# The first product of a row block pair in seven smaller ones, and a new order around it

## The chip, the cores and the metric

The kernel runs on one core of one Trainium2 chip. The metric is device time in microseconds of one execution; for the kernel before it is the median of three runs, 787.54 us (787.51 to 788.31). A separate execution was recorded by the hardware profiler; all durations below come from that one.

## The reference

Four sequences of 768 rows go through hash-bucketed attention (8 heads of 64), whose heads side by side are the 512 columns of x, and then through an MLP mixer:

```python
xt = x.transpose(0, 2, 1)
h = np.maximum(xt @ w_tok1, 0.0) @ w_tok2
u = x + h.transpose(0, 2, 1)
h2 = np.maximum(u @ w_ch1, 0.0) @ w_ch2      # 512 -> 1536 -> 512
return (u + h2).astype(np.float32)
```

Everything here concerns the first matrix product of the last step, u @ w_ch1, with the relu that follows. All data are float32.

## The kernel before

Attention fills the first 310 us, the token mixing runs to 388 us, and the rest is the channel part, `channels`. It works on XT, which holds u transposed: 128 partitions of columns by 4 blocks of columns by 3072 rows. The rows are taken in three row block pairs s = 0, 1, 2, each of two blocks of TT = 512 rows.

For each pair the product with w_ch1 is made by Winograd's form of a 2x2 block product: seven products p1 to p7 in place of eight, with sums of the blocks of the right side (the rows: T, made by `inputs`) and of the left side (the weights: SW1). For s = 1 and 2 most of the seven are themselves made in seven smaller ones. Class `Smaller` does that. Its `left` holds seven weight blocks of 128x128, its `b` eight blocks of 128x256 of the rows: four raw ones and four sums, which `right_sums` makes on VectorE with four subtractions. The seven matmuls of 256 columns come in three calls:

- `one(pair, e)`: one matmul into the first quarter of a pair of PSUM banks; `keep` copies it into `e` (ScalarE)
- `rest()`: three matmuls, of which the first adds onto that same quarter; `unite()` copies it again (ScalarE), and `add()` makes the other quarters (VectorE)
- `three(pair)`: three matmuls that go straight into the pair in which the whole product is wanted; `seed()` first copies the kept parts back into that pair (ScalarE)

`used()` runs after `three` and after `rest`, and when both are done, it asks for the next weight blocks of that product by a transfer on SP's queue.

The six blocks of 128 hidden columns of a row half are taken as three tiles t = 0, 1, 2 (GP = 3). `hidden_first(s, 0, ...)` does t = 0, `hidden_pair(s, t)` the others, then `outputs(s)` makes the product with w_ch2 by seven calls, `whole_product` and six of `product`, the last of them `product(s, 6, "p4", ...)`. All engines execute their instructions in the order in which these functions list them; there is no scheduler. A pair of PSUM banks is a tile with one buffer, taken anew by `bank_pair(i)`; there are four, whose order `ring` holds. `product` takes the first two of the ring and moves them to its end, so that `hidden_first` finds the pairs of the last product but one as x and z, and those of the last product as e and y.

Before, p1 for t = 0 is not made in smaller products: `opened` (L1036) makes it with four matmuls of 512 columns into X, and only its later tiles are `Smaller`, begun ahead by `open_next`. Their left sums are made once, by `sum_first_left` (L897) at the end of the third `product` of s = 0.

The right sums for a pair are made on VectorE: those of p2 and p3 already within `outputs(s - 1)`; those of p5 and p6 ahead of `hidden_first`; those of p7, p4 and p1 inside it, where it calls `between[0]` to `between[2]`. The lines that call it:

```python
for s in range(1, last + 1):
    for name in ("p5", "p6"):
        right_sums(name, s)[0]()
    hidden_first(s, 0, [right_sums(name, s)[0] for name in ("p7", "p4", "p1")])
```

A look (`look`, or `begin_look` and `end_look`) is work from another part of the kernel that is spread over these stages: two passes of ScalarE over 128x768 numbers of an input, which POOL's queue then follows with the load of a next one.

Of the kernel before, what the change touches and what calls it, by code (L numbers as in the profile page):

```python
# [48 lines left out]
def kernel(  # L49
# [705 lines left out]
    def channels(pool, psum, SW1, second, TA, judge):  # L755
# [15 lines left out]
        def bank_pair(i):  # L771
            return psum.tile([P, 2, TT], F32, name=f"b{i}", tag=f"b{i}", bufs=1)
# [7 lines left out]
        def accumulate(ps, left, right, ks, start=True, stop=True):  # L780
            ks = list(ks)
            for k in ks:
                nc.tensor.matmul(  # L783
                    ps, left(k), right(k), start=start and k == ks[0], stop=stop and k == ks[-1],
                    skip_group_check=True,
                )
# [101 lines left out]
        def fifth_left():  # L888
            return SW1[:, 1].rearrange("p k c -> p (k c)")[:, 2 * TT : 2 * TT + 4 * P]

        def first_left_sums():

            return [
                SW1[:, ::2].rearrange("p i k c -> p i (k c)")[:, :, P * (7 + i) : P * (8 + i)] for i in range(4)
            ]

        def sum_first_left():  # L897
            (a00, a01), (a10, a11) = [
                [a[:, 0, P:].rearrange("p (t c) -> p t c", c=P) for a in half]
                for half in weight_quarters(first_weight("p1"))  # L900
            ]
            new = first_left_sums()
            nc.vector.tensor_tensor(new[1], a00, a10, op=ALU.subtract)
            nc.vector.tensor_tensor(new[0], a10, a11, op=ALU.add)
            nc.vector.tensor_tensor(new[2], new[0], a00, op=ALU.subtract)
            nc.vector.tensor_tensor(new[3], a01, new[2], op=ALU.subtract)

        def hidden_left_at(h):

# [5 lines left out]
        def weight_quarters(w):  # L915
            k, c = w.shape[1] // 2, w.shape[2] // 2
            return [[w[:, :k, cs], w[:, k:, cs]] for cs in (slice(0, c), slice(c, 2 * c))]

        def first_weight(name):

            return {
                "p2": WC1[:, KC:, : DCH // 2], "p3": SW1[:, 2], "p4": WC1[:, KC:, DCH // 2 :], "p6": SW1[:, 0],
                "p5": WC1[:, :KC, DCH // 2 :], "p7": SW1[:, 1], "p1": WC1[:, :KC, : DCH // 2],
            }[name]
# [5 lines left out]
        class Smaller:  # L930


            def __init__(self, h, name, s, t):
                self.h, self.name, self.s, self.t, self.fetched = h, name, s, t, False
                self.b = right_sums(name, s)[1]
                if h is None:
                    raw = [a for b in weight_quarters(first_weight(name)) for a in b]
                    raw = [raw[i][:, 0, P * t : P * t + P] for i in (0, 1, 3)]
                    if name == "p1":
                        sums = [a[:, t - 1] for a in first_left_sums()]  # L940
                    else:
                        sums = [fifth_left()[:, P * i : P * i + P] for i in range(4)]
                    self.left = [*sums, *raw]
                else:
                    w = hidden_left_at(h).rearrange("p (i c) -> p i c", i=7)
                    self.left = [w[:, i] for i in range(7)]
# [75 lines left out]
        def plus(to, a, b):  # L1022
            nc.vector.tensor_tensor(to, a, b, op=ALU.add)  # L1023
# [4 lines left out]
        def relu(a):  # L1028
            nc.scalar.activation(a, a, ACT.Relu)

        def whole(pair, left, right, which, t):
            for i in which:
                at = P * (t + GP * i)
                accumulate(pair[:, i], lambda k: left(k)[:, at : at + P], right, range(KC))

        def opened(pair, which, s, t):  # L1036
            start = TT * 2 * s
            whole(pair, lambda k: WC1[:, k], lambda k: XT[:, k, start : start + TT], which, t)

        def open_next(bank, s, t):  # L1040
            p1 = Smaller(None, "p1", s, t + 1)
            p1.pair = bank_pair(bank)
            p1.one(p1.pair, left_at(7 * s + 1)[:, 2 * TT : 4 * TT])
            ahead.append(p1)

        def bounds(r):
# [10 lines left out]
        def hidden_first(s, t, between):  # L1057


            r, (p2, p6, p7, p3, p4) = parts_of(s, t)  # L1060
            x, z, e, y = ring
            ring[:] = [y, e, z, x]
            p1, e4, e2, e3 = [flat(output_at(i)) for i in range(4)]
            e7 = flat(q1)
            e5, e6, u = copies(), copies(), copies()
            p5 = Smaller(None, "p5", s, t)
            n = TT * 3 // 2

            X = bank_pair(x)
            opened(X, [0, 1], s, t)  # L1070
            look()
            Z, E = bank_pair(z), bank_pair(e)
            p2.one(E, e2)
            copy_pair(p1, X)
            p2.three(Z, True)
            Y = bank_pair(y)
            p5.one(Y, e5)
            begin_look()
            plus(p1[:, :n], flat(Z)[:, :n], p1[:, :n])
            between[0]()  # L1080
            p2.rest()
            p2.unite()
            end_look()
            p2.add()
            p5.rest()
            p5.unite()
            p5.add(True)
            p6.three(X)
            p6.one(bank_pair(z), e6, False)
            copy_pair(u, X)  # L1090
            p6.keep()
            p5.seed()
            plus(r[0], rows(p1), rows(e2))
            V = bank_pair(e)
            between[1]()
            p7.three(V, True)
            p6.rest()
            p6.finish()
            plus(u, u, e6)
            p7.one(bank_pair(x), e7)  # L1100
            p5.three(Y)
            p5 = e5
            copy_pair(p5, Y)
            p7.rest()
            plus(p5[:, :n], flat(V)[:, :n], p5[:, :n])
            p7.finish()
            p3.one(bank_pair(z), e3)
            p3.three(Y)
            relu(r[0])
            p4.three(V)  # L1110
            p4.one(bank_pair(x), e4)
            p3.rest()
            plus(r[1], banks(Y), rows(u))
            plus(u, u, e7)
            plus(r[2][:, 0], banks(V)[:, 0], rows(u)[:, 0])
            plus(r[2][:, 1, 0], banks(V)[:, 1, 0], rows(u)[:, 1, 0])
            between[2]()
            p3.finish()
            nc.scalar.copy(r[2][:, 1, 1], rows(u)[:, 1, 1])
            open_next(y, s, t)  # L1120
            p4.rest()
            p4.finish()
            later(1, "p6", lambda: plus(r[3], rows(p5), rows(u)))
            later(1, "p3", lambda: plus(r[1], r[1], rows(e3)))
            later(1, "end", lambda: relu(r[3]))
            later(2, "p2", lambda: plus(r[2], r[2], rows(e4)))
            later(2, "u", *bounds(r))
            later(2, "end", lambda: relu(r[2]))
# [105 lines left out]

        SMALLER = ["p2", "p6", "p7", "p3", "p4"]
        GP = HC // 2
        ahead, postponed, slots, finished = [], [], {}, [0]
        hidden_passed = second["hidden_passed"]


# [85 lines left out]
        def left_at(g):  # L1326
            return area(g % 2)[:, : 7 * QC * P]
# [143 lines left out]
        def outputs(s):  # L1471
# [45 lines left out]
            if s < last:  # L1517
                product(s, 5, "p2", q2, [
                    *end, right_sums("p2", s + 1)[0],
                ], [  # L1520
                    right_sums("p3", s + 1)[0],
                    *([lambda h=h: fetch_hidden_left(h) for h in range(5)] if s == 0 else []),
                ])
                product(s, 6, "p4", q4, [
                    add(q2, q2, q1), store(q2, 0, 0),
                ], [
                    lambda: inputs(s + 1, T, 0), lambda: inputs(s + 1, T, 1),
                ])
                add(q4, q4, q7)()
                store(q4, 1, 0)()  # L1530
            else:
                def final(at):
                    start = sl[0].start
                    def block(i, n=0, count=2):
                        return out[at + i, :, start + TT // 2 * n : start + TT // 2 * (n + count)]

                    return block

                product(s, 5, "p2", q1, [
                    *end, add(q1, q1, XT[:, :KC, sl[0]]),  # L1540
                ], [], final(0))
                product(s, 6, "p4", q7, [], [], final(KC))
# [79 lines left out]
        assert not jobs  # L1622
        outputs(0)
        for s in range(1, last + 1):
            for name in ("p5", "p6"):
                right_sums(name, s)[0]()
            hidden_first(s, 0, [right_sums(name, s)[0] for name in ("p7", "p4", "p1")])
            residual(s)
            for t in range(1, GP):
                hidden_pair(s, t)  # L1630
            outputs(s)
# [123 lines left out]
```

## Time and profile before

| what | us |
|---|---|
| median of three runs | 787.54 |
| the profiled execution | 788.62 |
| its span, first to last instruction | 786.8 |
| TensorE busy | 780.8 |
| VectorE busy | 666.4 |
| ScalarE busy | 481.1 |
| `hidden_first`, s = 1: 524.25 to 546.26 | 22.01 |
| `hidden_first`, s = 2: 653.04 to 675.05 | 22.01 |

Times in the trace count from the first instruction of the span. A row of the timeline has its start, the time that it and the rows merged with it cover, the engine (PE is TensorE, PEld its weight loads, DVE VectorE, ACT ScalarE, SPq and POOL the queues), the line, the operation with what it writes and reads, and in brackets the idle time of the engine just before it and what ended it. A float32 matmul is two records with two weight loads. A line can be that of a helper: all matmuls here are L783.

### The profile page before, as it was taken

The page shows a single profiled execution, that of the slowest core. Times are in us where ns is not written, and L with a number is a line of the kernel's source. Part 1 is how long each engine was busy: PE and PEld are TensorE (multiplying, and loading weights), DVE is VectorE, ACT ScalarE, POOL GpSimd, SP SyncE. Part 2 cuts the span into 40 slices and gives each one's busy share as a digit, 9 for nine tenths or more (in the row PEclk, how much of TensorE's full clock was granted, in tenths as well). Part 3 has the DMA queues.
Part 4 walks back from the last instruction along what each step waited for, and adds up shares of the span by engine and source line. Part 5 has one row for each costly group of instructions (what it writes and reads, how often), then busy time and mean ns, then how long its engine had stood idle before and what let it go on. Part 6 is the DMA issues. An engine that isn't in the chain of part 4 may idle for free.

```text
span 786.8 us, 12638 instructions
## 1 busy us (share of the span) xinstructions
PE 780.8 (99%) x4757; PEld 483.0 (61%) x4757; DVE 666.4 (85%) x910; ACT 481.1 (61%) x831; POOL 53.5 (7%) x77
## 2 busy tenths in 40 slices
PE   9999999999999999999999999999999999999997
PEld 5444444444444444455544448888887887886886
DVE  5989898989887677999787889889899798889884
ACT  6688888888888887333323225655784666665331
POOL 1000000000000000011121010120000122000001
PEclk9999999999999999999999999999999999999999
DMA  4435353537352425796596997797766687650565
GB/s 165 164 123 164 124 164 124 164 123 244 124 171 91 132 86 174 201 264 135 101 278 222 297 376 276 231 284 203 238 218 210 245 242 184 189 170 1 187 167 133
DMA packets 102530, 145.40 MB, mean 185 GB/s; under 512 B 30200, under 2 KB 72640, under 8 KB 102464
## 3 DMA queue, kind: packets, MB, share of 16 engines
q1 hardware_dynamic: 94448, 119.68, 46.4%
q0 software_dynamic: 7728, 24.64, 13.6%
q8 instruction: 39, 0.64, 0.3%
q14 instruction: 27, 0.22, 0.1%
q10 hardware_dynamic: 288, 0.21, 0.1%
HBM read 101.53 MB, written 35.52 MB: 174 GB/s over the span
## 4 chain that ended last, share of the span: by engine, by line
PE 99%; DVE 0%; issue 0%; DVEq 0%
PE b L783 50%; PE sc L356 20%; PE acc L410 16%; PE t L656 5%; PE t L696 5%; PE sums L434 2%; PE hp L301 1%; PE idle L473 0%; PE hw L325 0%; DVE second L1023 0%; DVE ones L97 0%; PE b L1598 0%; DVEq L1750 0%
## 5 line engine op out<-in xcount | busy, mean ns | idle before, releaser
L363 ACT ACTIVATE e<-sc 128x768 f32<-128x768 f32 x192 | 154.5, 810 | 6.6 <-PE sc L356 6.2
L356 PE MATMUL sc<-qk 64*128 64x384 f32 x768 | 153.3, 485 | 0.0
L783 PE MATMUL b<-R,second 128*128 128x256 f32 (+1 forms) x522 | 131.9, 409 | 0.0
L410 PE MATMUL acc<-e,vn 128*32 128x384 f32 x1536 | 127.0, 486 | 0.0
L783 PEld LDWEIGHTS b<-R,second 128*128 128x128 f32 x522 | 99.0, 190 | 28.7 <-issue 16.5
L395 DVE TENSOR_TENSOR esd<-esd,e 128x768 f32<-128x768 f32 x96 | 92.0, 958 | 10.4 <-ACT e L363 0.5
L410 PEld LDWEIGHTS acc<-e,vn 128*32 128x32 f32 x1536 | 49.9, 110 | 73.9 <-issue 73.5
L356 PEld LDWEIGHTS sc<-qk 64*128 64x128 f32 x768 | 68.5, 188 | 42.3 <-issue 38.1
L789 ACT COPY c<-b 128x256 f32<-128x256 f32 (+1 forms) x96 | 40.2, 425 | 79.4 <-PE b L783 68.9
L783 PE MATMUL b<-XT,WC 128*128 128x256 f32 (+1 forms) x212 | 65.0, 444 | 0.0
L356 PE MATMUL sc<-bits 64*128 64x384 bf16 x384 | 62.5, 323 | 0.0
L783 PEld LDWEIGHTS b<-XT,WC 128*128 128x128 f32 x212 | 40.1, 190 | 19.2 <-issue 14.9
L391 DVE SCALAR_TENSOR_TENSOR esd<-e 128x768 f32<-128x768 f32 x32 | 30.6, 955 | 23.4 <-ACT e L363 23.4
L783 PE MATMUL b<-XT,SW 128*128 128x256 f32 (+1 forms) x164 | 46.7, 410 | 0.0
L656 PE MATMUL t<-x,W 128*128 128x512 f32 x96 | 41.8, 593 | 0.0
L356 PEld LDWEIGHTS <-bits 64*128 64x128 bf16 x384 | 18.6, 94 | 32.9 <-issue 9.6
L783 PEld LDWEIGHTS b<-XT,SW 128*128 128x128 f32 x164 | 31.1, 190 | 9.4 <-issue 4.1
L416 ACT ACTIVATE num<-acc,vsum 128x384 f32<-128x384 f32 x32 | 18.6, 581 | 29.8 <-PE acc L410 29.4
L716 POOL DMA_DIRECT2D XT<-second x8 | 9.9, 1234 | 383.5 <-DVE second L715 355.8
L455 ACT COPY rec<-rec 32x384 f32<-32x384 f32 x64 | 32.6, 510 | 5.0 <-DVE rec L449 4.2
L398 DVE TENSOR_TENSOR esd<-esd,e 128x768 f32<-128x768 f32 x32 | 30.5, 954 | 1.9
L656 PEld LDWEIGHTS t<-x,W 128*128 128x128 f32 x96 | 18.2, 190 | 22.7 <-issue 21.3
(255 smaller groups left out, 1272.3 us busy)
## 6 DMA issues: line engine op xcount, KB each, us to landing
second<-left SPq DMA_DIRECT2D x20, 768.0 KB
raw<-in_moe_w_ch SPq DMA_DIRECT2D x16, 768.0 KB
qk<-in_qk SPq DMA_DIRECT2D x15, 768.0 KB
second<-left SPq DMA_DIRECT2D x18, 576.0 KB
seen<-in_qk POOLq DMA_DIRECT2D x21, 384.0 KB, 5.5
WC<-hidden_left SPq DMA_DIRECT2D x18, 448.0 KB
vn<-in_v SPq DMA_DIRECT2D x16, 384.0 KB
vt<-in_vT SPq DMA_DIRECT2D x16, 384.0 KB
```

Source lines behind the costliest of these rows:

```text
L356: nc.tensor.matmul(sc[:, i, :HALF], t[rows, 1, P * c : P * c + P], t[rows, 0, qs], start=start, stop=not start,)
L363: nc.scalar.activation(e, sc[:, :, :HALF], ACT.Exp, scale=SCALE)
L391: nc.vector.scalar_tensor_tensor(self.d, es[0], NR * EPS, es[1], op0=ALU.add, op1=ALU.add,)
L395: nc.vector.tensor_tensor(self.d, self.d, e, op=ALU.add)
L398: nc.vector.tensor_tensor(self.d, self.d, self.es[-1], op=ALU.add)
L410: nc.tensor.matmul(acc[D * i + d : D * i + d + 32], vn[:, i, c, d : d + 32], e[:, i], start=(c == 0), stop=(c == NR - 1),)
L416: nc.scalar.activation(nums[self.n][:, self.half], acc, ACT.Identity, scale=-1.0, bias=vsum,)
L455: nc.scalar.copy(rec[other : other + 32, h], rec[at : at + 32, h])
L656: nc.tensor.matmul(ps, W1[:, r, P * j : P * j + P], x[:, r], start=(r == 0), stop=(r == NR - 1),)
L696: nc.tensor.matmul(ps[at], left, right, start=start, stop=True, skip_group_check=True,)
L783: nc.tensor.matmul(ps, left(k), right(k), start=start and k == ks[0], stop=stop and k == ks[-1], skip_group_check=True,)
L789: nc.scalar.copy(c, ps)
```

## The change

- p1 for t = 0 is now a `Smaller` as well (`first`). Its four left sums are made by `sum_first_left`, which now runs over the first column tile and the two others; they are kept in free ends of SW1 and WC1.
- p5's right sums are made in the preceding product, between the two halves of `inputs`; p1's at the beginning of the pair; p7's, p6's and p4's later in it.
- The last addition and store of `outputs(s - 1)`, q4, are put on a list, `closing`, and done within `hidden_first` after p1's right sums.
- The order within `hidden_first` is new: it begins with p2's single product in bank pair e and p1's in x.

```diff
-        def first_left_sums():
+        def first_left_sums(first):
+            if first:
+                tails = [SW1[:, i].rearrange("p k c -> p (k c)")[:, 11 * P : 12 * P] for i in (0, 2)]
+                more = WC1[:, KC:].rearrange("p k c -> p (k c)")[:, 21 * P : 23 * P]
+                return [a.rearrange("p (t c) -> p t c", c=P) for a in (*tails, more[:, :P], more[:, P:])]
...
         def sum_first_left():
-            (a00, a01), (a10, a11) = [
-                [a[:, 0, P:].rearrange("p (t c) -> p t c", c=P) for a in half]
...
+            for first, columns in ((True, slice(0, P)), (False, slice(P, GP * P))):
+                (a00, a01), (a10, a11) = [
+                    [a[:, 0, columns].rearrange("p (t c) -> p t c", c=P) for a in half]
...
+        def first_place(s):
+            return left_at(7 * s + 1)[:, 2 * TT : 4 * TT]
...
-            p5 = Smaller(None, "p5", s, t)
+            first, p5 = Smaller(None, "p1", s, t), Smaller(None, "p5", s, t)
             n = TT * 3 // 2
 
-            X = bank_pair(x)
-            opened(X, [0, 1], s, t)
+            X, Z, E, Y = [bank_pair(i) for i in (x, z, e, y)]
+            p2.one(E, e2)
+            first.one(X, first_place(s))
+            between[0]()
+            for work in closing.pop():
+                work()
+            p2.three(Z, True)
             look()
-            Z, E = bank_pair(z), bank_pair(e)
-            p2.one(E, e2)
-            copy_pair(p1, X)
-            p2.three(Z, True)
-            Y = bank_pair(y)
-            p5.one(Y, e5)
-            begin_look()
-            plus(p1[:, :n], flat(Z)[:, :n], p1[:, :n])
-            between[0]()
+            first.rest()
+            first.unite()
+            between[1]()
+            first.add(True)
             p2.rest()
             p2.unite()
-            end_look()
             p2.add()
+            p5.one(Y, e5)
+            first.seed()
             p5.rest()
             p5.unite()
+            first.three(X)
+            copy_pair(p1, X)
+            between[2]()
             p5.add(True)
+            V = bank_pair(e)
+            p7.three(V, True)
+            plus(p1[:, :n], flat(Z)[:, :n], p1[:, :n])
+            p5.seed()
+            plus(r[0], rows(p1), rows(e2))
             p6.three(X)
             p6.one(bank_pair(z), e6, False)
             copy_pair(u, X)
             p6.keep()
-            p5.seed()
-            plus(r[0], rows(p1), rows(e2))
-            V = bank_pair(e)
-            between[1]()
-            p7.three(V, True)
+            p5.three(Y)
+            between[3]()
+            p5 = e5
+            copy_pair(p5, Y)
             p6.rest()
             p6.finish()
+            p7.one(bank_pair(x), e7)
+            look()
+            p3.three(Y)
+            plus(p5[:, :n], flat(V)[:, :n], p5[:, :n])
             plus(u, u, e6)
-            p7.one(bank_pair(x), e7)
-            p5.three(Y)
-            p5 = e5
-            copy_pair(p5, Y)
             p7.rest()
-            plus(p5[:, :n], flat(V)[:, :n], p5[:, :n])
             p7.finish()
             p3.one(bank_pair(z), e3)
-            p3.three(Y)
             relu(r[0])
             p4.three(V)
+            plus(r[1], banks(Y), rows(u))
+            p3.rest()
+            p3.unite()
             p4.one(bank_pair(x), e4)
-            p3.rest()
-            plus(r[1], banks(Y), rows(u))
             plus(u, u, e7)
             plus(r[2][:, 0], banks(V)[:, 0], rows(u)[:, 0])
             plus(r[2][:, 1, 0], banks(V)[:, 1, 0], rows(u)[:, 1, 0])
-            between[2]()
-            p3.finish()
+            p3.add()
             nc.scalar.copy(r[2][:, 1, 1], rows(u)[:, 1, 1])
             open_next(y, s, t)
             p4.rest()
...
-                    lambda: inputs(s + 1, T, 0), lambda: inputs(s + 1, T, 1),
+                    lambda: inputs(s + 1, T, 0), right_sums("p5", s + 1)[0], lambda: inputs(s + 1, T, 1),
                 ])
-                add(q4, q4, q7)()
-                store(q4, 1, 0)()
+                closing.append([add(q4, q4, q7), store(q4, 1, 0)])
...
-            for name in ("p5", "p6"):
-                right_sums(name, s)[0]()
-            hidden_first(s, 0, [right_sums(name, s)[0] for name in ("p7", "p4", "p1")])
+            hidden_first(s, 0, [right_sums(name, s)[0] for name in ("p1", "p7", "p6", "p4")])
```

More of the change, by code (lines that the diff above doesn't have):

```diff
@@ L897, in sum_first_left @@
         def sum_first_left():
-            (a00, a01), (a10, a11) = [
-                [a[:, 0, P:].rearrange("p (t c) -> p t c", c=P) for a in half]
[L900 to L906, printed above, removed]
+            for first, columns in ((True, slice(0, P)), (False, slice(P, GP * P))):
+                (a00, a01), (a10, a11) = [
+                    [a[:, 0, columns].rearrange("p (t c) -> p t c", c=P) for a in half]
+                    for half in weight_quarters(first_weight("p1"))
+                ]
+                new = first_left_sums(first)
+                nc.vector.tensor_tensor(new[1], a00, a10, op=ALU.subtract)
+                nc.vector.tensor_tensor(new[0], a10, a11, op=ALU.add)
+                nc.vector.tensor_tensor(new[2], new[0], a00, op=ALU.subtract)
+                nc.vector.tensor_tensor(new[3], a01, new[2], op=ALU.subtract)
         def hidden_left_at(h):
@@ L939, in __init__ @@
                     if name == "p1":
-                        sums = [a[:, t - 1] for a in first_left_sums()]
+                        sums = [a[:, max(t - 1, 0)] for a in first_left_sums(t == 0)]
                     else:
@@ L1029, in relu @@
             nc.scalar.activation(a, a, ACT.Relu)
[L1031 to L1038, printed above, removed]
+        def first_place(s):
+            return left_at(7 * s + 1)[:, 2 * TT : 4 * TT]
         def open_next(bank, s, t):
@@ L1042, in open_next @@
             p1.pair = bank_pair(bank)
-            p1.one(p1.pair, left_at(7 * s + 1)[:, 2 * TT : 4 * TT])
+            p1.one(p1.pair, first_place(s))
             ahead.append(p1)
@@ L1236, in channels @@
         GP = HC // 2
-        ahead, postponed, slots, finished = [], [], {}, [0]
+        ahead, closing, postponed, slots, finished = [], [], [], {}, [0]
         hidden_passed = second["hidden_passed"]
```

## The prediction

> **What bounds the kernel now.** I read the page's engine list and chain first, then the two stages that the change rewrites as windows, then those stages in order of time, engine by engine. The page:
>
> ```profile
> PE 780.8 (99%) x4757; PEld 483.0 (61%) x4757; DVE 666.4 (85%) x910; ACT 481.1 (61%) x831; POOL 53.5 (7%) x77
> ...
> PE 99%; DVE 0%; issue 0%; DVEq 0%
> ```
>
> TensorE ends the program nearly everywhere. A busy TensorE need not be a full one, so I looked at the stage itself. The windows are the two first row block pairs (columns: length, then each engine's busy time):
>
> ```profile
> core 0: us, PE busy (x) PEld busy (x) DVE busy (x) ACT busy (x) POOL busy (x), PEclk, DMA share, GB/s
> 524.25:546.26 22.01, 22.01 (x96) 17.86 (x95) 19.90 (x37) 12.99 (x25) 2.36 (x3) 1.00 0.85 217
> 653.04:675.05 22.01, 22.01 (x96) 17.87 (x95) 19.75 (x36) 12.99 (x25) 2.82 (x4) 1.00 0.73 192
> ```
>
> Both last 22.01 us. Their matmuls are 4 of 512 columns and 43 of 256. One matmul is two records, and in the trace a record starts 0.429 us after the one before at 512 columns and 0.216 us at 256. So 4 x 0.858 + 43 x 0.431 = 21.97: there is no idle time here to win. Any gain has to be removed matmuls; any new wait of TensorE is paid in full.
>
> What a wait costs comes from the timeline. First the head of the stage, TensorE then ScalarE:
>
> ```profile
> 524.25 5.32 PE L783 MATMUL b<-XT,WC 128*128 128x512 f32 x16
> 529.41 0.59 PE L783 MATMUL b<-TA,WC 128*128 128x256 f32 x2
> 529.85 1.46 PE L783 MATMUL b<-XT,WC 128*128 128x256 f32 x6
> ...
> 524.46 0.37 ACT L789 COPY second<-b 128x256 f32<-128x256 f32 x1 [1.29 <-PE b L783]
> 528.32 0.37 ACT L956 COPY second<-b 128x256 f32<-128x256 f32 x1 [1.69 <-PE b L783]
> 530.05 0.37 ACT L956 COPY c<-b 128x256 f32<-128x256 f32 x1 [0.44 <-PE b L783]
> ```
>
> The matmul at 529.41 is p5's single product; its copy runs from 530.05 to 530.42. So a product is copied out 0.64 + 0.37 = 1.01 us after its start. Then the one place where TensorE did wait for a copy in these stages:
>
> ```profile
> 650.48 0.84 ACT L1568 ACTIVATE seen<-seen 128x768 f32<-128x768 f32 x1 [0.65 <-DMA seen<-in_qk]
> ...
> 651.23 0.35 ACT L789 COPY c<-b 128x256 f32<-128x256 f32 x1
> ...
> 651.63 1.16 PEld L783 LDWEIGHTS b<-R,second 128*128 128x128 f32 x6 [0.30 <-ACT c L789]
> ```
>
> The copy ended at 651.583, the weight load that waited began at 651.635, 0.05 later. The records before and after it (651.359, 651.957) stand 0.598 apart instead of 2 x 0.215, so 0.17 us was lost, and the held matmul began in effect 0.11 after its load. From the start of a product to the earliest start of a matmul that overwrites it: 1.01 + 0.05 + 0.11 = **1.17 us**. In the order of before at least 1.29 us of other matmuls stands in every such place.
>
> [...]
>
> **The change part by part**, for one of the two pairs (s=1 and s=2).
>
> *p1.* Removed: 4 x 0.858 = 3.43. Added: one, three, rest = 7 x 0.431 = 3.02. **-0.41**.
>
> *Head.* p2's single product is now TensorE's first instruction. It goes into bank pair e, the pair A of the product just ended, whose last reader is the copy at 524.46 (ring: the last product's A and B are its third and fourth entries). A pair has one buffer, so its first matmul waits for all readers of the old contents, although this one lies in the other bank of the pair. In before the same weight load (527.26) carries a wait for ScalarE too, long satisfied. Now the copy ends at 524.83, the load starts at 524.88 and the matmul at 524.99 instead of 524.25: **+0.73**. All of TensorE queues behind it. At s=2 the copy is at 653.24 after 653.04: the same. Bounds: 0 if the wait is only for the bank written, 0.8 if the copy is late.
>
> *p5.* p5's single product is followed on TensorE by p5.rest at once; first.seed between them is ScalarE's. rest begins by accumulating onto the bank that the copy reads: 1.17 - 0.43 = **+0.74**. ScalarE is free then: p2's last copy ended about 0.9 us earlier. Bounds: 0.7 to 0.9.
>
> *p4.* Before, p3.rest and the next p1 product stood between p4.one and p4.rest (1.72 us); now only the latter: 1.17 - 0.43 - 0.43 = **+0.31**. Bounds: 0.2 to 0.5.
>
> *X.* p6.three adds onto X, which the 1.02 us copy of p1 reads. That copy begins 0.64 after p1's third added matmul, so p6.three is free 0.86 + 0.64 + 1.02 + 0.16 = 2.68 after p1.three began; p1.three and p7.three cover 6 x 0.431 = 2.59: **+0.09** (0 to 0.2).
>
> Elsewhere the cover holds. first.rest needs p1's copy: p2.three's 1.29 covers 1.17 - 0.43. p6.rest needs p6's copy, behind a copy of X: free 2.95 after p6.three began, 3.02 covered. p6.one needs Z read: 0.25 to spare. p3.three, p4.three, p7.rest: 0.2 us or more.
>
> *VectorE.* It loses p5's four sums from the stage (before 526.00 to 527.54, 1.54 us) and gains first.add (0.68 + 0.42, about 1.05 from start to start): less work in a longer stage. p1's sums have a deadline: first.rest's load at T + 2.15 - 0.21 + 0.73 = T + 2.67, T being 524.25. p5's sums now lie between the two halves of inputs, where VectorE idled 1.09 us for the transfer that freed TB; they take 1.54, so all behind moves 0.45 and VectorE is free at 524.86. p1's third sum, 1.09 later, ends at T + 1.70: 0.97 to spare, and 0.24 if the head wait does not come.
>
> *Left sums.* Four ops of about 0.29 us in the third product of s=0 delay begin, whose first result was ready at 493.15 and is used at 498.4. Nothing.
>
> *Queues.* POOL: the store of q4 comes behind p1's sums, but was issued only at 529.81, when the store before it had landed (529.47); its add now ends near 527.5. At s=2 the add ends near 656.1, where the store stood (656.12). The two looks each issue a load, some 2 and 10 us later; only the next looks use them. SP: p5's next lefts are now asked for ahead of p6's; p6's fetch moves from 536.95 to about 539.4 and is used near 547.7. 448 KB at the stage's 217 GB/s takes 2.1 us. p2's lefts are used 3.4 us earlier at s=1, at 524; their 896 packets of 512 B had begun by 520.
>
> Sum for a pair: -0.41 + 0.73 + 0.74 + 0.31 + 0.09 = **+1.46**; two pairs: **+2.92**. The profiled execution took 788.62 us (span 786.8 and 1.8 around it), so 791.5 for that one; it lies 1.1 above the median of the three runs, 787.54, so the median becomes **790.4**. Of this the two head waits are 1.46, p5's 1.48, p4's 0.62.
>
> **The rivals.** 0.2% is 1.57 us, about what a measurement of this kernel can tell from no change.
>
> Head wait absent (the one that ends not slower): the place is p2's product at the stage's beginning, the price 0.73 a pair. Without it 2 x (1.46 - 0.73) = +1.46 remains: 789.0, just inside 0.2%. It decides from 0.67 us a pair down (2.92 - 1.57, halved). For it: the copy reads the other bank. Against it: the wait that the load already carries, and that one buffer serves both.
>
> Only the matmuls count: every wait hidden, -0.82 in all: 786.7. For it: TensorE waits almost nowhere today. Against it: p5.rest behind p5.one has no matmul in between at all.
>
> More waits: VectorE, busy 19.90 of 22.01, or a fetch gets late; 0.5 to 2 us a pair, about 792.5. For it: margins of 0.07 and 0.25 us. Against it: the waits above give VectorE time.
>
> Faster by over 0.2% would need 1.57 us out of stages where 0.82 of matmuls and the 0.17 at 651.6 are all there is.
>
> **How the numbers follow.** Chances: forecast 0.76, head wait absent 0.08, only the matmuls 0.05, more waits 0.09, anything faster 0.02. The forecast's own range is 789.5 to 791.3 (the bounds of the four waits and 0.3 us of run to run). The range for 8 in 10 runs from 788.7 to 791.9: it takes in most of the head-wait rival and the lower part of "more waits". Within 0.2%: 0.05 + 0.05 + 0.02 from the forecast's low end = 0.12; slower 0.86; faster 0.02.
>
> **What would show it.** The stage should last 23.5 us instead of 22.01, with four gaps before weight loads: about 0.73 at its beginning released by the copy of L789, 0.74 before p5.rest and 0.31 before p4.rest released by the copies of L956, under 0.2 before p6.three. A stage of 22.7 with no gap at the head is the first rival; 21.6 the second; gaps released by VectorE or a transfer the third. The product before each pair should still end without a gap. I am wrong if ScalarE's copies start much sooner after a product than 0.64 us, or if the head's wait is finer than the pair.

## The result, and the profile after

The changed kernel takes 791.74 us (median of 6 runs, 791.07 to 792.30), the kernel before beside it 787.71 (6 runs, 787.51 to 788.32): ratio 1.0049, 95% interval 1.0036 to 1.0062. It is slower, by more than the 0.2% that can be told from no change. The time lies in the predicted range (788.7 to 791.9), near its upper end and 1.3 above the predicted 790.4. The profiled execution took 792.16 us, with a span of 790.4.

The page of the changed kernel, its engine list and the first line of its chain:

```profile
PE 781.6 (99%) x4769; PEld 484.2 (61%) x4769; DVE 669.2 (85%) x918; ACT 484.8 (61%) x837; POOL 53.7 (7%) x77
...
PE 99%; DVE 0%; ACT 0%; issue 0%; DVEq 0%
```

TensorE still ends the program. It has only 0.8 us more busy time than before in a span that is 3.5 us longer; so most of what was added lies outside its busy time. The two stages as windows (length, then each engine's busy time and instructions, granted clock, DMA share, GB/s), from the end of the product before to the first load of `hidden_pair`:

```profile
524.04:547.50 23.46, 22.51 (x102) 18.67 (x101) 20.42 (x38) 14.74 (x28) 2.36 (x3) 1.00 0.83 212
654.28:677.75 23.47, 22.51 (x102) 18.68 (x101) 20.43 (x38) 14.74 (x28) 2.39 (x3) 1.00 0.65 175
```

Before, both stages had 22.01 us, all of it busy. Now there are 50 matmuls of 256 columns, 21.58 us (with one more at the border they make the 102 records); the other 1.9 us is waiting, of which the profile counts 0.93 as busy time (22.51). Where it is, the weight loads of the changed kernel in order of time show (start, busy time, what is loaded for; in brackets the idle time before it and what released it):

```profile
524.75 2.02 PEld L783 LDWEIGHTS b<-XT,WC 128*128 128x128 f32 x10 [0.86 <-ACT second L789]
...
530.66 1.16 PEld L783 LDWEIGHTS b<-second,SW 128*128 128x128 f32 x6 [0.86 <-ACT c L961]
...
534.68 0.73 PEld L783 LDWEIGHTS b<-TB,WC 128*128 128x128 f32 x4 [0.26 <-ACT second L1031]
...
546.20 1.16 PEld L783 LDWEIGHTS b<-XT,SW 128*128 128x128 f32 x6 [0.43 <-ACT second L961]
```

They are p2's single product at the head, p5.rest, p6.three and p4.rest, each released by a copy of ScalarE. The bracket counts from the end of the load before, which is ahead of its matmul anyway (by 0.22 us at the load of 526.80 and its matmul at 527.02); what TensorE loses is read from the starts of its matmul records, each against the 0.216 us that a 256-column record takes otherwise. So counted, the four cost 0.73, 0.73, 0.13 and 0.30 us, in both pairs to 0.01 (the expectations below have 0.10 for the third, which leaves out 0.03 us that it loses before its load). The copies in front of the first two, on ScalarE:

```profile
524.33 0.37 ACT L789 COPY second<-b 128x256 f32<-128x256 f32 x1 [1.29 <-PE b L783]
...
530.24 0.37 ACT L961 COPY c<-b 128x256 f32<-128x256 f32 x1
```

The first ends at 524.70, and the held load begins 0.05 later; the second ends at 530.61, and the load again 0.05 later. ScalarE is not late with either of them: the product that it copies is simply too recent. The first reads the second bank of its pair and p2's product goes into the first bank; its load waited all the same.

From its first matmul to its last, the part of the program with these stages takes 396.98 us on TensorE, against 394.08 in the first trace of before: 2.89 more. The two stages are 2.95 longer, the rest 0.06 shorter; in the rest, a wait of 0.17 that only before's trace has and one of 0.18 that only this one has cancel out (both are taken up below).

### The profile page after: what moved, and what is told of

Its sections match the earlier page's. It is cut to its first block, busy times and chain, and to the rows that moved or that the text cites. A ratio compares the mean times of both kernels' runs of the same rounds, so it can differ in the third digit from the quotient of the medians.

```text
span 790.4 us, 12675 instructions
## 1 busy us (share of the span) xinstructions
PE 781.6 (99%) x4769; PEld 484.2 (61%) x4769; DVE 669.2 (85%) x918; ACT 484.8 (61%) x837; POOL 53.7 (7%) x77
## 4 chain that ended last, share of the span: by engine, by line
PE 99%; DVE 0%; ACT 0%; issue 0%; DVEq 0%
PE b L783 50%; PE sc L356 20%; PE acc L410 16%; PE t L656 5%; PE t L696 5%; PE sums L434 2%; PE hp L301 1%; PE idle L473 0%; PE hw L325 0%; DVE bits L337 0%; ACT c L961 0%; ACT second L789 0%; DVE bits L330 0%; DVE second L1028 0%; DVE ones L97 0%
## 5 line engine op out<-in xcount | busy, mean ns | idle before, releaser
L789 ACT COPY c<-b 128x256 f32<-128x256 f32 (+1 forms) x96 | 40.3, 426 | 79.4 <-PE b L783 69.2
L783 PE MATMUL b<-XT,WC 128*128 128x256 f32 (+1 forms) x208 | 61.2, 429 | 0.9 <-ACT second L789 0.9
L656 PEld LDWEIGHTS t<-x,W 128*128 128x128 f32 x96 | 18.2, 190 | 22.7 <-issue 21.3
```

The source lines that it names most:

```text
L656: nc.tensor.matmul(ps, W1[:, r, P * j : P * j + P], x[:, r], start=(r == 0), stop=(r == NR - 1),)
L783: nc.tensor.matmul(ps, left(k), right(k), start=start and k == ks[0], stop=stop and k == ks[-1], skip_group_check=True,)
L789: nc.scalar.copy(c, ps)
```

## The experiments

Three groups: the waits one by one, what lies behind them, and whether the saved matmuls can be had at all. "Stage" is the first pair's length on TensorE, from the end of the product before to where the first matmul of `hidden_pair` effectively starts, by the spacing of the records; where the second pair differs by over 0.1, both stand. "TensorE" is the growth of the whole part over its 393.91 us in the second trace of before (which lacks the 0.17 us wait at 651.63). The medians of the kernel before beside each are between 788.07 and 788.25.

| kernel | stage us | TensorE us | median us | ratio, 95% interval |
|---|---|---|---|---|
| b_again (before) | 22.00 | 0 | 787.83 | 1.0000, 0.9992 to 1.0008 |
| a_again (changed) | 23.47 | +3.07 | 791.63 | 1.0045, 1.0032 to 1.0059 |
| e1_head | 22.74 | +1.61 | 789.87 | 1.0024, 1.0016 to 1.0032 |
| e2_p5 | 22.88 | +1.89 | 790.41 | 1.0030, 1.0021 to 1.0039 |
| e3_p4 | 23.47 | +3.07 | 791.54 | 1.0042, 1.0028 to 1.0056 |
| e4_all | 22.56 | +1.24 | 789.82 | 1.0024, 1.0016 to 1.0032 |
| e5_direct | 23.04 | +2.21 | 790.98 | 1.0041, 1.0026 to 1.0055 |
| e8_bank | 23.47 | +3.07 | 791.65 | 1.0046, 1.0033 to 1.0060 |
| e6_clear | 22.95, 22.80 | +1.88 | 790.74 | 1.0037, 1.0024 to 1.0051 |
| e9_pool | 23.86, 23.43 | +3.24 | 791.19 | 1.0040, 1.0027 to 1.0054 |
| e10_less | 22.02 | +0.02 | 788.56 | 1.0007, 0.9999 to 1.0015 |
| e11_less | 23.47 | +3.07 | 791.94 | 1.0049, 1.0036 to 1.0063 |

### The waits one by one

**The head** (e1_head): p2's single product goes behind p1's and p2's three added ones.

```diff
-            p2.one(E, e2)
             first.one(X, first_place(s))
...
             p2.three(Z, True)
+            p2.one(E, e2)
```

> Of the changed kernel, p2's single product is moved behind p1's single product and p2's three, so that 1.7 us of other matmuls stand before the first use of bank pair e. My theory (that product waits for the copy which reads the pair last): the gap of 0.73 us at the head of hidden_first goes, the stage lasts 22.7 us instead of 23.46, the whole 1.46 us less than the changed kernel, about 790.3. Rival (the head waits for something else, as VectorE's sums for p1, or the product only moves the wait): a gap of the same size appears before p1.rest or before p2's product, no gain.

The loads of e1_head run through the head of the stage; p5.rest's wait is untouched:

```profile
523.85 2.13 PEld L783 LDWEIGHTS b<-XT,WC 128*128 128x128 f32 x10
...
529.87 1.16 PEld L783 LDWEIGHTS b<-second,SW 128*128 128x128 f32 x6 [0.86 <-ACT c L961]
```

Stage 22.74: exactly the 0.73 a pair is gone, and nothing took its place. Half of what the change costs is the place of this one instruction. p1's sums on VectorE, due 0.73 us earlier here, were still in time.

**The head, one matmul in between** (e5_direct): p1's single product, then p2's at once.

```diff
-            p2.one(E, e2)
             first.one(X, first_place(s))
+            p2.one(E, e2)
```

> At the head p1's single product first, then p2's single product at once, before p2.three. Theory (the wait ends with the copy, 0.73 us after the stage's begin, whatever stands before it): one matmul of 0.43 covers part of it, the gap is 0.73 - 0.43 = 0.30 us, the stage 23.46 - 0.43 = 23.03 us, 0.86 us faster than the changed kernel, 790.8. Rival (a wait costs a fixed time, however long TensorE had been busy before): gap 0.73, stage 23.46 us, 791.6.

```profile
523.63 0.41 PEld L783 LDWEIGHTS b<-XT,WC 128*128 128x128 f32 x2
524.47 1.59 PEld L783 LDWEIGHTS b<-XT,WC 128*128 128x128 f32 x8 [0.43 <-ACT second L789]
```

The gap is 0.30 us to the hundredth, the stage 23.04. The wait has no fixed price: what counts is that 1.17 us of other matmuls stand between a product's start and the matmul that overwrites it, and each matmul put in between pays its full 0.43.

**p5** (e2_p5): its single product goes ahead of p2.rest.

```diff
             first.add(True)
+            p5.one(Y, e5)
             p2.rest()
...
-            p5.one(Y, e5)
             first.seed()
```

> Of the changed kernel, p5's single product is moved ahead of p2.rest, so that 1.29 us of matmuls stand between it and p5.rest. My theory (a product can be overwritten 1.17 us after its start): the gap of 0.73 us before p5.rest goes, the stage lasts 22.7 us, the whole 1.46 us less, about 790.3. Rival (p5.rest is held by ScalarE's other copies or by VectorE's sums): the gap stays or shrinks by less than half.

p5.rest runs without a gap, but the stage is 22.88, not 22.7. The next thing to be late shows in its loads:

```profile
531.48 0.73 PEld L783 LDWEIGHTS b<-XT,WC 128*128 128x128 f32 x4 [0.27 <-ACT b L1010]
```

This is p1's three added products (`first.three`), which want the seed that ScalarE copies at L1010. It cost 0.14 us; while p5.rest waited, that was covered.

**p4** (e3_p4): its single product goes ahead of p3.rest.

```diff
+            p4.one(bank_pair(x), e4)
             p3.rest()
             p3.unite()
-            p4.one(bank_pair(x), e4)
```

> Of the changed kernel, p4's single product is moved ahead of p3.rest, as it stood before the change, so that 1.72 us of matmuls stand between it and p4.rest. My theory: the gap of 0.30 us before p4.rest goes, the stage lasts 23.16 us, the whole 0.6 us less, about 791.1. Rival: bank pair x is not yet read by then (p7's additions end 0.1 us ahead by my count), and a gap appears before the product instead, no gain.

Nothing was won, 23.47. In e3_p4 the load before p4.rest has no gap, but p4's single product itself does:

```profile
543.35 0.30 PEld L783 LDWEIGHTS b<-TB,SW 128*128 128x128 f32 x2 [0.42 <-issue]
```

It loses 0.28 us. The profile names no releaser. p4.one takes a new bank pair in x, whose last reader is VectorE's second addition of p7:

```profile
542.81 0.42 DVE L1003 TENSOR_TENSOR q<-b,q 128x256 f32<-128x256 f32 x1
```

It ends at 543.23, 0.12 before the load. So I take the wait to be for this one; the same 0.12 stands in e4_all (542.99 and 543.10). So the move by three matmuls (1.29 us) was 0.28 us too far, where 0.30 us were wanted. From these numbers I estimate that a move by one or two matmuls (0.43 or 0.86 us) has neither wait; e9_pool and e10_less below move it by one, and there neither comes.

**All three** (e4_all).

> All three moves together. If the waits simply add, the stage lasts 21.7 us (21.60 of matmuls and 0.10 before p6.three), 0.3 us less than before the change, and the whole is 3.5 us under the changed kernel, about 788.2. My theory says less: p1's additions on VectorE end 5.9 us after the stage begins whatever TensorE does, the seed copy after them 6.8, so that p1.three now waits 0.5 us; stage 22.2 us, the whole 2.6 us under the changed kernel, about 789.2: still not faster than before the change.

Stage 22.56. The additive expectation fell, and the other named the right wait, with the right size, but missed p4.one's (the first load is first.three's, the second p4.one's):

```profile
531.04 0.73 PEld L783 LDWEIGHTS b<-XT,WC 128*128 128x128 f32 x4 [0.64 <-ACT b L1010]
...
543.10 0.30 PEld L783 LDWEIGHTS b<-TB,SW 128*128 128x128 f32 x2 [0.41 <-issue]
```

first.three loses 0.50, p4.one 0.28, p6.three 0.13, p5.rest 0.04: 0.95 in place of 1.89. The three waits taken out were worth 1.76 a pair, and 0.85 of it came back. The seed's way on the traces: first.add ended at 530.10, since the copy that it needs ran from 528.57 to 528.92, behind both halves of a look. VectorE had ended p7's right sums at 528.62 and stood idle for the 0.33 us until that copy was done; so the look held the seed up, and without it p7's sums would have, 0.33 us less.

### What lies behind them

**The other bank first** (e8_bank). p5.rest and p4.rest begin with the matmul whose bank the copy doesn't read.

```diff
-            def rest(self):
+            def rest(self, other_bank=False):
+                if other_bank:
+                    self.mm(self.ps[:, 2], 1, 5)
                 self.mm(self.ps[:, 0], 2, 6, False)
                 self.mm(self.ps[:, 1], 0, 4, False)
-                self.mm(self.ps[:, 2], 1, 5)
+                if not other_bank:
+                    self.mm(self.ps[:, 2], 1, 5)
...
-            p5.rest()
+            p5.rest(True)
...
-            p4.rest()
+            p4.rest(True)
```

> p5.rest and p4.rest of the first pairs begin with the matmul into the other bank of the pair (ps[2]), the two into the bank that the copy reads behind it. Theory (inside one opened pair a matmul waits only for readers of what it writes): one matmul of 0.43 us now stands in each wait, p5.rest's gap 0.73 becomes 0.30, p4.rest's 0.30 becomes 0; stage 23.46 - 0.73 = 22.73 us, 1.46 us faster than the changed kernel, about 789.7. Rival (the wait is for the whole pair, as at the head): gaps stay, 23.46 us, 791.1.

```profile
530.62 1.16 PEld L783 LDWEIGHTS b<-second,SW 128*128 128x128 f32 x6 [0.86 <-ACT c L961]
...
546.16 1.16 PEld L783 LDWEIGHTS b<-XT,SW 128*128 128x128 f32 x6 [0.43 <-ACT second L961]
```

Both gaps stay as they were. My theory fell: in this program not only a newly opened pair waits as a whole (0.73 us at the head), a pair already in use does too (0.73 us at p5.rest and 0.30 at p4.rest, with the matmul into the other bank first). On the reader's side it is the same, in the changed kernel too: p5.unite begins 1.60 us after p5.rest does, 0.64 after the last of its three matmuls began, which goes into the other bank, though it reads what the first one wrote.

**VectorE taken off the changed kernel** (e11_less). The addition of q7 to q4, 1.13 us of VectorE at the stage's beginning (to the start of the next instruction; its own length is 1.22), is left out; with it a part of the output of the first two rows.

```diff
-                closing.append([add(q4, q4, q7), store(q4, 1, 0)])
+                closing.append([store(q4, 1, 0)])
```

> The changed kernel with the addition of q7 to q4 left out (a part of the output of the first two rows is then not computed), its order untouched. Theory (its four waits are for ScalarE's copies, and VectorE has time): the same 1.1 us of VectorE's work that decides in e10 is worth nothing here, gaps 0.73, 0.73, 0.10 and 0.30 as before, stage 23.46 us, 791.6. Rival (VectorE is behind the waits, the copies waiting for its results): stage shorter by 0.3 us or more, 791.0 or below.

VectorE falls from 20.43 to 19.28 us in the window, and the stage doesn't move (changed kernel first, then e11_less):

```profile
524.13:547.60 23.47, 22.52 (x102) 18.77 (x101) 20.43 (x38) 14.74 (x28) 2.36 (x3) 1.00 0.83 213
```

```profile
523.74:547.20 23.46, 22.50 (x101) 18.77 (x101) 19.28 (x37) 14.74 (x28) 2.36 (x3) 1.00 0.82 212
```

So the waits are not for VectorE. They are for copies that are waiting for TensorE themselves: in the changed kernel's first trace the one at 524.33 by its bracket, the one at 530.24 by its start, 0.63 us after that of its product.

**Both kernels again** (a_again, b_again), unaltered.

> The changed kernel, unaltered. Its channel part on TensorE was 2.89 us longer than before's, its median 4.03 us above. Theory (the four waits and the smaller p1 are all; the rest is scatter of the program's end and of the few runs): about 791.1, 3.0 above the kernel before, stage again 23.46 us and channel part +2.9; the time from the last matmul to the end differs from its 6.06 us in the first trace by tenths, in either direction. Rival (the change also lengthens the program's end): 4.0 above, and again about 6.06 us after the last matmul.

> The kernel before, unaltered, for a second trace and as a measure of what a comparison can tell. 788.1, ratio 1.000. Stage 22.01 us both times, channel part 394.08 us. Theory: the time from the last matmul to the end (5.28 us in the first trace) and the start of the channel part (387.47) move by tenths from one execution to the next. Rival: they are the same to 0.1 us, and so belong to the kernel.

The stages repeat to 0.01 us, and TensorE's part of the changed kernel to 0.001 (396.975 and 396.976). Before had 394.08 and then 393.91: the wait of 0.17 us at 651.63 hung on a look's transfer and did not come a second time. A wait of 0.18 us, in the product p2 of s=1 (at 630.95), is in both traces of the changed kernel and in neither of before; it too is released by a copy of L789. It is in eight more of the versions here, and missing in e9_pool and e10_less alone. Why that copy is late is not shown.

From the start of the last matmul to the end the two traces of before took 5.28 and 5.13 us, those of the changed kernel 6.06 and 5.43. So this end scatters by over half a microsecond for one kernel. In the twelve traces of changed kernels here it is 5.25 to 6.23, 5.71 in the mean. Whether the change has a part in that, two traces of before can't settle; but in the table the medians, too, lie above those of before by 0.1 to 0.8 us more than TensorE's growth, in all changed versions except e9_pool. Up to the issue of the last store (0.87 us after the last matmul's start) all traces agree to 0.01; SP's last wait for that store, of 128 KB, then ends 3.58 us after that start in the first trace of before and 4.36 in the first of the changed kernel. The rest of the end, 1.70 us, is the same in all. What makes the store slower is not shown.

### Can the saved matmuls be had

**e6_clear**: the order of e1 and e2, the look's halves put where ScalarE idles, p7's right sums behind first.add, p4.rest begun in the other bank.

```diff
-            p2.one(E, e2)
             first.one(X, first_place(s))
+            begin_look()
...
             p2.three(Z, True)
-            look()
+            p2.one(E, e2)
             first.rest()
             first.unite()
-            between[1]()
+            end_look()
             first.add(True)
+            between[1]()
+            p5.one(Y, e5)
             p2.rest()
...
-            p5.one(Y, e5)
             first.seed()
...
-            p4.rest()
+            p4.rest(True)
```

> The order of e1 and e2 together, with the look's two halves put where ScalarE idles (after first.one, and after first.unite), p7's right sums put behind first.add, and p4.rest begun in the other bank. Theory: in e4 first.three waited 0.50 us for its seed, because the copy of first.rest stood behind the look and first.add behind p7's sums; with both out of the way only p6.three's 0.10 is left: stage 22.01 - 0.41 + 0.10 = 21.7 us, about 787.5, 0.6 below before. Rival (VectorE's total work sets the seed, or p6.three and p6.one wait on VectorE instead): stage 22.0 us or more, 788.1 or above.

It missed: 22.95. The wait for the seed is gone, as foreseen, and the rival's came in its place. The load of p6's single product and the additions before it, on VectorE:

```profile
534.74 0.30 PEld L783 LDWEIGHTS b<-TB,WC 128*128 128x128 f32 x2 [0.73 <-DVE second L1031]
```

```profile
532.68 0.69 DVE L1003 TENSOR_TENSOR c<-b,second 128x512 f32<-128x512 f32 x1
533.40 0.43 DVE L1006 TENSOR_TENSOR b<-b,c 128x256 f32<-128x256 f32 x1
533.74 0.95 DVE L1031 TENSOR_TENSOR second<-b,second 128x768 f32<-128x768 f32 x1
```

p6.one needs Z read, and 533.74 is that reading (the addition to p1). VectorE has worked without a pause since 527.63; it came 0.60 us late. Smaller gaps stand at first.rest (0.15, for p1's sums, in the first pair alone), p5.rest (0.19, its copy behind the look's second half), p6.three (0.13) and p4.rest (0.30, as e8 says).

**e9_pool** takes the 1.13 us of q4's addition to GpSimd, and is to mend the smaller gaps. The lines are against the changed kernel, those at the head that it shares with e6 left out.

```diff
-                closing.append([add(q4, q4, q7), store(q4, 1, 0)])
+                closing.append([lambda: nc.gpsimd.tensor_tensor(q4, q4, q7, op=ALU.add), store(q4, 1, 0)])
...
-            first.rest()
+            first.rest((1, 2, 0))
             first.unite()
             between[1]()
             first.add(True)
+            between[2]()
+            p5.one(Y, e5)
+            first.seed()
             p2.rest()
             p2.unite()
             p2.add()
-            p5.one(Y, e5)
-            first.seed()
+            end_look()
             p5.rest()
...
-            between[2]()
...
-            p3.rest()
-            p3.unite()
+            p3.rest((0, 1), False)
             p4.one(bank_pair(x), e4)
+            p3.rest((2,))
+            p3.unite()
```

> e6 taken further: q4's addition on GpSimd instead of VectorE, p6's right sums straight behind first.add, the look's second half behind p2.unite, first.rest in the order in which its sums get ready, and p4.one one matmul ahead of p3.rest's end. Theory (VectorE, unbroken from 527.6 to 534.7 in e6, is what holds p6.one; with 1.13 us taken off it the sum for p6.one ends near 533.4, before it is wanted): the waits of e6 go, only p6.three's 0.10 stays, stage 22.01 - 0.41 + 0.10 = 21.7 us, about 0.6 below before: 787.4. Rival (the addition on GpSimd is slow, or slows VectorE beside it, and the copy into p1 waits for it, or another wait of ScalarE or VectorE opens): stage 22.0 us or more, 788.0 or above.

It missed, with 23.86 us, and 23.43 in the second pair; the rival's first reason came true:

```profile
524.53 0.41 DVE L859 TENSOR_TENSOR second<-XT 128x256 f32<-128x256 f32 x1
...
524.76 2.40 POOL L1538 TENSOR_TENSOR second<-second 128x1024 f32<-128x1024 f32 x1 [1.19 <-ACT second L961]
524.86 2.58 DVE L860 TENSOR_TENSOR second<-XT 128x256 f32<-128x256 f32 x1
...
527.36 0.41 DVE L861 TENSOR_TENSOR second<-XT,second 128x256 f32<-128x256 f32 x1
527.49 0.30 PEld L783 LDWEIGHTS b<-second,SW 128*128 128x128 f32 x2 [1.43 <-DVE second L860]
```

The addition took GpSimd 2.40 us, about twice VectorE's 1.22, and in that time VectorE finished nothing: p1's second sum, begun 0.1 us after the addition, has 2.58 us, the ones on either side 0.41, and it ends 0.28 us after GpSimd's end. TensorE waits 1.30 us for it. In the second pair the two take 2.65 and 2.57 us, and TensorE waits 0.73 us. The profile names nothing that held VectorE up; that it was the addition on GpSimd I take from these times, and from e10_less below, where without that addition TensorE has no wait there. Further gaps of 0.3 to 0.4 us follow in both pairs: at first.three for its seed, at p7.three, and at the first product of `hidden_pair`.

**e10_less** is e9 with that addition left out altogether (and with it a part of the output of the first two rows).

```diff
-                closing.append([lambda: nc.gpsimd.tensor_tensor(q4, q4, q7, op=ALU.add), store(q4, 1, 0)])
+                closing.append([store(q4, 1, 0)])
```

> e9 with the addition of q7 to q4 left out altogether, on GpSimd and on VectorE (a part of the output of the first two rows is then not computed). Theory (VectorE's work is what keeps the reordered stage from showing the saved matmuls): e9's waits for VectorE and for the seed all go, stage 22.01 - 0.41 + 0.10 = 21.7 us, about 0.6 below before: 787.5. Rival (ScalarE's copies hold the stage too): stage 22.0 us or more, 788.1.

Stage 22.02 (22.06 in the second pair): 0.9 better than e6, and no better than before. The seed, p5.rest, p6.three, p6.one and p4.rest all come without a gap. What took the 0.41 us is a gap of 0.13 before p7.three (0.18 in the second pair), and this one before the first product of `hidden_pair`:

```profile
546.09 0.30 PEld L783 LDWEIGHTS b<-TB,WC 128*128 128x128 f32 x2 [0.43 <-PE b L783]
```

```profile
542.42 1.21 DVE L1028 TENSOR_TENSOR R<-b,c 128x1024 f32<-128x1024 f32 x1
543.66 1.22 DVE L1028 TENSOR_TENSOR c<-c,q 128x1024 f32<-128x1024 f32 x1
544.99 1.02 DVE L1028 TENSOR_TENSOR R<-b,c 128x512 f32<-128x512 f32 x2
```

It costs 0.30 us. That product opens the pair V, which VectorE's last two additions here read until 546.02, 0.07 before the load; they stand behind p7's and two long ones. p7.three is much the same: it opens the pair that p2.add reads until 531.91, 0.07 before its load, and p2.add stands behind p6's right sums. The profile names other releasers, TensorE and a copy of ScalarE. That it is VectorE is read from the order and these times; no run took it away. So even with 1.1 us less for VectorE than the computation needs, the stage is as long as before. The median, 788.56, is 0.4 above its neighbours of before, with TensorE's part the same; that is inside the interval, and of the size of what e10_less spends more at its end (5.47 us from the last matmul's start). No version here beats the kernel before.

## Why the prediction was right

**The sum on TensorE was right, term by term.** Predicted and measured, for one pair: p1 -0.41 and -0.42 (50 of 256 columns where 4 of 512 and 43 of 256 stood); head +0.73 and +0.73; p5 +0.74 and +0.73; p4 +0.31 and +0.30; X +0.09 and +0.13. Together +1.46 and +1.47. The rule behind three of them, 1.17 us from a product's start to a matmul that overwrites it, held also where a run put it to the test with another spacing (e5_direct, 0.30 us). The four new 128x128 subtractions, put at about 0.29 us, took 0.28 to 0.29 us each; the step between 256 and 768 columns in the trace of before (0.42 and 0.95 us) gives 0.29 for them as well.

**One reading of p5's term was off, without harm.** The prediction had ScalarE free for p5's copy, p2's last copy having ended about 0.9 us earlier. In the changed kernel it ended 0.06 us earlier, at 530.18:

```profile
529.81 0.37 ACT L995 COPY second<-b 128x256 f32<-128x256 f32 x1 [0.92 <-PE b L783]
530.24 0.37 ACT L961 COPY c<-b 128x256 f32<-128x256 f32 x1
```

The copy at 529.81 is p2.unite, which starts 0.64 after the third matmul of p2.rest and not after the first, whose result it reads. With a copy longer than the 0.43 us of one matmul the term would have come out larger; that it came out at 0.73 is in this part luck.

**The step on the unit of the wait was right.** The head wait is for the pair, not the bank (0.73 us, though its copy reads the other bank); this was the rival's opening. e1_head shows the price by taking it away, 0.73 us, and e8_bank that a pair in use is waited for as a whole as well (0.73 and 0.30 us as before).

**The rival "more waits"** was wrong in its place: VectorE holds nothing up in the changed kernel (e11_less). Its reason was sound: the small margins that the prediction read, 0.25 us for p6.one and 0.24 for p1's sums without the head wait, are what gives way once the waits are taken out (0.60 us in both pairs, and 0.15 in the first, in e6_clear).

**"Only the matmuls"** fell with the four gaps. The runs add why its 0.82 us were not had by moving products: the head's wait went without another in its place, but with p5's or p4's product moved, or several at once, the next copy or addition was 0.1 to 0.6 us late. That no order at all could have them is not shown.

**The time was 1.3 us short**, and the term that was mis-sized is the step from the profiled execution to the median. The prediction made its sum against 788.62 and got 791.54; that is 0.2 from the measured median. The forecast took 1.1 us off that, since the profiled execution lay that far above the median of three runs. The 100 runs of the kernel before in these comparisons have their median at 788.07, so 0.5 would have been right for that. The rest of the miss is 0.18 us for the wait at 630.95, which the prediction had not seen (it counts in full only if before's other runs lack the 0.17 at 651.63, as one of its two traces does), and about 0.5 us at the end of the program: 5.71 us in the mean from the last matmul's start against 5.2. These three make 1.2. The cause of the wait at 630.95 and of the last part stays open; the last can't be TensorE, which has finished, and the scatter of a single kernel (6.06 and 5.43) is as large as the difference.

The forecast's own range, 789.5 to 791.3, did not hold the median of 791.74. The wider one did, by 0.2 us, because it left room for the lower part of "more waits" in the two stages. That is not what happened, so that it held is partly luck.

## What to carry to other kernels

Where TensorE has no idle time, a product that is copied out and then accumulated on, or whose buffer is opened again, needs a full turnaround of other matmuls in between: start of the product to end of its copy plus the restart, 1.17 us here. Count that distance for every place whose neighbours an order changes, before counting what the change saves.

A wait taken out can uncover the next: price it by the margin of what is late next, and not by its own size alone. Of the three taken out here one by one, the head's was worth its full 0.73 us, p5's 0.59, p4's nothing. And take an execution's excess over the median of a few runs as scatter of both, not as a constant to be carried over.

## What the runs showed of the hardware

- An f32 addition of 128x1024 on GpSimd took 2.40 us, and a 128x256 subtraction of VectorE that began 0.1 us after it took 2.58 us instead of 0.41 (e9_pool; 2.65 and 2.57 in the second pair).
- A load that was held by a copy of ScalarE begins 0.05 us after the copy's end, and its matmul in effect 0.10 to 0.11 after that (so at all four places in both pairs of the changed kernel's first trace, and at 651.63 in that of before); behind an addition or subtraction of VectorE the load came 0.05 to 0.12 us after its end (0.05 in e6_clear and e9_pool, 0.12 in e3_p4).
- While the load at 524.75 of the changed kernel was held, TensorE ran nothing that stands behind it: its records have no matmul between 523.91 and 524.75. p1's single product stood behind it and did not need that copy: put ahead of it, in e5_direct, its loads ran through at 523.63.
- Between two executions of one kernel (the first trace of the changed kernel and a_again) the time from the last matmul's start to the end was 6.06 and 5.43 us, with TensorE's part of the channel stage and the issue of the last 128 KB store after it the same to 0.01 us.
